# A decode step over a cached window, bound by its loads: sums of half heads, one bank for value products, constants from GpSimd

## The chip, the cores and the metric

The kernel runs on one core of one Trainium2 chip. The metric is device time in microseconds (us) per execution, the median of three runs; a separate execution is profiled. TensorE (PE) multiplies matrices into PSUM, a memory of eight banks with 512 fp32 words per partition each; VectorE (DVE), ScalarE (ACT) and GpSimd (POOL) work elementwise; SyncE (SP) issues nearly all DMAs, in its program's order. Engines wait for each other through semaphores (`wait_ge`).

## What is computed

For a batch of B = 4, one new token each, D = 640, 32 heads of Dh = 192, and the last W = 2048 of 8192 cached positions:

```python
xn  = layernorm(x)
q   = (xn @ wq) per head
k, v = k_cache[:, :, -W:, :], v_cache[:, :, -W:, :]
o   = softmax(q k^T * Dh**-0.5) v          # per batch row and head
out = x + o @ wo + (silu(xn @ w1) * (xn @ w3)) @ w2
```

All inputs are bf16. K and V of the window are 3.1 MB per head each, some 200 MB in all; each element of them is used once.

## The kernel before

**Layout.** The 128 partitions hold 32 groups of positions for each of the 4 batch rows; a head's K tile is 128 x 64 positions x 192. There are two K buffers `kt`, two V buffers `vt`, one buffer `prs` for products of K and q with two halves, and eight PSUM banks: `ps` 0 and 1, `o_ps` 0 and 1, `mt`, `tb`, `po`, `acc`.

**Start.** SP loads W_q (into the V buffers and `prs`), w1, w3, w2, K0 and K1 without waiting (L172 to L179). GpSimd makes two identity matrices (L207 to L213). VectorE makes the constants `one`, `tot_w`, `sel_w`, `mask` (L226 to L243), then the layernorm; through the helper `dv` each of its operations waits for the one before. PE projects q for all heads into six banks, VectorE and ScalarE copy it to `qbc` (L257 to L263, L345 to L348); then come the gated MLP's products, with the gate in `tb` (L405 to L420).

**One head h.** VectorE multiplies K with q in two halves (`mult`, L274), 128 x 6144 each. Per quarter of a head PE adds up the 192 products in six matmuls of 512 columns with the identity (`adder`, L422), which leaves 16 positions x 32 partial sums in one bank, and VectorE sums the 32 (`reduce_quarter`, L280). Then follow for the softmax: the maximum per partition (`chain_lmax`, L285), a transpose on PE (`tr`, L434), the maximum per batch row (`chain_gmax`, L289), its negative on ScalarE (L353), a matmul that spreads it over the partitions (`bc`, L438), its copy and the exponential with row sums on ScalarE (L355, L357), the weights times a batch mask (`chain_z`, L294), a matmul that sums the row sums (`tot`, L443), and 32 matmuls with V (`pv`, L447). ScalarE copies the value product out (L360); `osum` (L458) collects it into `po`, two heads together, and VectorE scales it by the reciprocal (`norm_rec` and `norm_og`, L299 and L302), for every second head. `proj` (L464) multiplies by W_o into `acc`.

**Order.** Every engine's order is written out by hand. On VectorE, per head h (L310 to L325): `mult(h,0)`, the last two quarters of head h-1, `lmax(h-1)`, `mult(h,1)`, `gmax(h-1)`, the first two quarters of head h, for odd heads the reciprocal and the scaling of an earlier pair, `z(h-1)`. On PE, per head (L489 to L498): `adder(0)`, `tr(h-1)`, `osum(h-2)`, `adder(1)`, `bc(h-1)`, `adder(2)`, `tot(h-1)`, `pv(h-1)`, `adder(3)`. The first and third `adder` wait for a reduce that follows the product on VectorE (`s_pr`). The heads at both ends are written out (L470 to L483 and L501 to L543).

**Loads.** SP alternates K(h+2) and V(h+1) (L181 to L183). K(h+2) waits until both products of head h are made (`s_m`, L159), V(h+1) until the value product of head h-1 is made (`s_pv`, L165). The last ones are K30, K31, V29, V30, V31 in two parts (L190 to L194), and behind them the last rows of W_o, into the first K buffer, in four pieces, the last of them 160 KB (L195 to L200).

Of the kernel before, what the change touches and what calls it, by code (L numbers as in the profile page):

```python
# [16 lines left out]
def kernel(  # L17
# [95 lines left out]
    ps = [psum(f"ps{i}", [P, QC], FP32) for i in range(2)]  # L113
    o_ps = [psum(f"o_ps{i}", [P, QC], FP32) for i in range(2)]
    mt = psum("mt", [P, QC], FP32)
    tb = psum("tb", [P, QC], FP32)
# [3 lines left out]
    def sem(name):  # L120
# [4 lines left out]
     s_gp, s_dv, s_ac, s_pp, s_m, s_ps, s_red, s_tr, s_gmax, s_bc, s_negm, s_exp, s_pv, s_sum, s_rec, s_og, s_oT,  # L125
     s_tot, s_acc) = [sem(n) for n in (
        "s_x", "s_wq0", "s_wq1", "s_wq2", "s_w1", "s_w3", "s_w2", "s_k0", "s_k1", "s_v31", "s_wom", "s_wo5",
        "s_wo6", "s_wo7a", "s_wo7b", "s_gp", "s_dv", "s_ac", "s_pp", "s_m", "s_ps", "s_red", "s_tr", "s_gmax", "s_bc",
# [28 lines left out]
    def load_k(h):  # L157
        if h >= 2:
            sp.wait_ge(s_m, 2 * (h - 2) + 2)  # L159
        sp.dma_start(out=flat(kt[h % 2]), in_=k_win[:, h].rearrange("b (p j) d -> p b (j d)", p=PB)).then_inc(s_k[h % 2], 16)  # L160
# [34 lines left out]
    sp.wait_ge(s_m, 2 * (H - 2) + 2)  # L195
# [18 lines left out]


# [3 lines left out]
    def dv(fn, *a, **k):  # L219
        if n_dv[0]:  # L220
            ve.wait_ge(s_dv, n_dv[0])
        fn(*a, **k).then_inc(s_dv, 1)  # L222
        n_dv[0] += 1
        return n_dv[0]

    dv(ve.memset, one[:], 1.0)  # L226
    dv(ve.memset, tot_w[:], 0.0)
    dv(ve.memset, sel_w[:], 0.0)
    dv(ve.memset, acc[:, 0:N0], 0.0)
# [3 lines left out]
    dv(ve.tensor_reduce, out=rows[:], in_=idf[:].rearrange("q (c k) -> q k c", k=CT)[:, 0:2 * B, :], axis=AX.X, op=ALU.add)  # L233
    PQ = CT // B

    def quads(t, par):
        return t.rearrange("p (s q r) b -> p s q r b", s=2, q=2)[:, :, par]

    for par in range(2):
        dv(ve.tensor_copy, out=quads(tot_w[:, par], par), in_=mask_f[:].unsqueeze(1).unsqueeze(1).to_broadcast([P, 2, PQ, B]))  # L240
        for k in range(2):
            dv(ve.tensor_copy, out=quads(sel_w[:, par, k], par),
               in_=rows[:, k * B:(k + 1) * B].unsqueeze(1).unsqueeze(1).to_broadcast([P, 2, PQ, B]))  # L243
    ve.wait_ge(s_x, 16)
    dv(ve.tensor_copy, out=xf, in_=x_sb[:])
# [4 lines left out]
    n_vpe = dv(ve.tensor_scalar, out=vpe[:], in0=ssq[:], scalar1=1.0 / D, scalar2=EPS, op0=ALU.mult, op1=ALU.add)  # L250
    ve.wait_ge(s_ac, 2)
    dv(ve.reciprocal, out=rstd[:], in_=std[:])
    n_xn = dv(ve.tensor_scalar_mul, out=xn[:], in0=xc, scalar1=rstd[:, 0:1])
    xnT_ps = tb[:, 0:KC * B // 2].bitcast(BF16).rearrange("p (k b) -> p k b", b=B)
    ve.wait_ge(s_pp, 1)
    n_xnT = dv(ve.tensor_copy, out=xnT[:], in_=xnT_ps.unsqueeze(2).to_broadcast([P, KC, PB, B]))
    q_banks = [ps[0], ps[1], o_ps[0], o_ps[1], mt, tb]  # L257
    n_qd = []
    for c0 in (0, 6):
        for i in (1, 3, 5):  # L260
            ve.wait_ge(s_pp, 1 + c0 + i + 1)
            n = dv(ve.tensor_copy, out=qbc[:, (c0 + i) * QC:(c0 + i + 1) * QC], in_=q_banks[i][:])
        n_qd.append(n)  # L263
    ve.wait_ge(s_ac, 2 + 6)
    for i in range(2):
        dv(ve.memset, o_ps[i][:, 0:2 * Dh], 0.0)
# [3 lines left out]
       in1=sT[:].rearrange("p (r c) -> p r c", c=FC), op=ALU.mult)  # L270
    n_hT = dv(ve.transpose, out=flat(hT), in_=flat(hb))

    def mult(h, a):
        if a == 0:  # L274
# [3 lines left out]
                         op=ALU.mult).then_inc(s_m, 1)  # L278

    def reduce_quarter(h, g):  # L280
        ve.wait_ge(s_ps, GQ * h + g + 1)
        ve.tensor_reduce(out=sc[h % 3][:, g * JQ:(g + 1) * JQ], in_=ps[g % 2][:].rearrange("p (j d) -> p j d", d=DD),  # L282
                         axis=AX.X, op=ALU.add).then_inc(s_red if g % 2 else s_pr, 1)
# [15 lines left out]
    def norm_rec(i):  # L299
        ve.reciprocal(out=rt[:], in_=tb[:, 0:1]).then_inc(s_rec, 1)  # L300

    def norm_og(i):  # L302
        sl = slice(i % 2 * 2 * CT, (i % 2 + 1) * 2 * CT)
        ve.wait_ge(s_rec, i + 1)
# [5 lines left out]
    for h in range(H):  # L310
        mult(h, 0)
        if h:
            reduce_quarter(h - 1, 2)
            reduce_quarter(h - 1, 3)
# [4 lines left out]
        reduce_quarter(h, 0)  # L319
        reduce_quarter(h, 1)  # L320
        if h % 2 and h > 1:
            norm_rec(h // 2 - 1)
            norm_og(h // 2 - 1)
        if h:
            chain_z(h - 1)  # L325
    reduce_quarter(H - 1, 2)
    reduce_quarter(H - 1, 3)
# [4 lines left out]
    norm_rec(NP - 1)  # L332
    ve.wait_ge(s_sum, H)
# [11 lines left out]
    for c0 in (0, 6):  # L345
        for i in (0, 2, 4):
            ae.wait_ge(s_pp, 1 + c0 + i + 1)
            ae.copy(out=qbc[:, (c0 + i) * QC:(c0 + i + 1) * QC], in_=q_banks[i][:]).then_inc(s_ac, 1)  # L348
    ae.wait_ge(s_pp, 14)
    ae.activation(out=sT[:], in_=tb[:, 0:FW], func=ACTF.Silu).then_inc(s_ac, 1)  # L350
    for h in range(H):
# [8 lines left out]
        ae.copy(out=o_sb[h % 2][:], in_=o_ps[h % 2][:, 0:2 * Dh]).then_inc(s_osb, 1)  # L360
# [28 lines left out]
    acc_add(idb[0:B, 0:B], x_sb[:], start=True)  # L389
    pe.wait_ge(s_dv, n_xnT)  # L390
    for c0 in (0, 6):
# [3 lines left out]
        for kc in range(KC):  # L395
# [4 lines left out]
            for i, qp in enumerate(q_banks):  # L400
                m = held(qp[:], w, wq_rows[kc][:, (c0 + i) * QC:(c0 + i + 1) * QC], kc == 0, kc == KC - 1)
# [3 lines left out]
    for t, bank, s in ((wts[0], tb, s_w1), (wts[1], mt, s_w3)):  # L405
        if bank is tb:
            pe.wait_ge(s_dv, n_qd[1])
        else:
            pe.wait_ge(s_ac, 2 + 6)
# [12 lines left out]
    def adder(g):  # L422
        if g % 2 == 0:
            take(pe, s_pr)
        add_up(g)

    def add_up(g):
        pe.ldweights(idb[:])  # L428
        pr = prs[:, g // 2, g % 2]
        for kk in range(NK):  # L430
            m = held(ps[g % 2][:].rearrange("p (j d) -> p j d", d=DD), idb[:], pr[:, :, kk * DD:(kk + 1) * DD], kk == 0, kk == NK - 1)
# [142 lines left out]
```

## Time and profile before

| what | before |
|---|---|
| median of 3 runs | 528.28 us (528.25 to 528.38) |
| the profiled execution | 528.51 us |
| its span | 525.7 us |
| DMA | 223.08 MB, mean 424 GB/s |
| PE busy | 358.6 us (68%), 2307 matmuls |
| VectorE busy | 342.0 us (65%), 360 instructions |
| ScalarE busy | 54.2 us (10%) |
| GpSimd busy | 1.1 us, 8 instructions |
| products of K and q (L276) | 64 x 3353 ns |
| sums of a quarter on VectorE (L282) | 128 x 681 ns |
| granted TensorE clock, mean | 0.86 |

The span is cut into 40 equal slices in the page; each digit of a strip is a busy share in tenths. A group's line gives the source line, engine, operation, the tiles it writes and reads, how often, the busy time, and the time that its engine sat idle ahead of it with what ended the idleness. A line of the timeline begins with start and duration in us. Where PE is busy at a low granted clock, the same matmuls take longer, so its busy time is no measure of its work.

### The profile page before, as it was taken

How to read it: one execution, taken by the hardware profiler on the slowest of the kernel's cores; microseconds unless marked ns; L12 is line 12 of the kernel's file. 1: busy time of each engine (PE TensorE's matmuls, PEld its weight loads, DVE VectorE, ACT ScalarE, POOL GpSimd, SP SyncE). 2: the span in 40 equal slices, each digit the busy share in tenths (PEclk: the TensorE clock that was granted, in tenths of full speed). 3: DMA queues.
4: the chain of work that ended last, by engine and by line, in shares of the span. 5: the costliest groups of instructions: out<-in, count | busy, mean ns of one | idle time of the engine just before them, and what ended most of it. 6: DMA issues, size and time to landing. Idle time of an engine off the chain costs nothing. (4 is left out here: it accounts for less than half of the span.)

```text
span 525.7 us, 4915 instructions
## 1 busy us (share of the span) xinstructions
PE 358.6 (68%) x2307; PEld 98.3 (19%) x1617; DVE 342.0 (65%) x360; ACT 54.2 (10%) x174; POOL 1.1 (0%) x8
## 2 busy tenths in 40 slices
PE   2664786667587267866767666877676667678697
PEld 0010121112121012211112111222121112222133
DVE  4135777777367574668767676667776766667961
ACT  2120110000111011110100111111010101111010
POOL 0000000000000000000000000000000000000000
PEclk9997888878869688797878888788797888887999
DMA  8999999999999999999999999999999999999995
GB/s 358 422 440 423 438 428 434 434 426 426 439 438 428 434 422 442 428 439 425 439 425 439 428 438 428 434 432 430 438 426 441 426 435 430 438 428 434 432 419 211
DMA packets 11521, 223.08 MB, mean 424 GB/s; under 512 B 1260, under 2 KB 1400, under 8 KB 2424
## 3 DMA queue, kind: packets, MB, share of 16 engines
q1 hardware_dynamic: 11496, 222.96, 98.8%
q8 instruction: 4, 0.07, 0.0%
q14 instruction: 5, 0.04, 0.0%
q10 hardware_dynamic: 16, 0.01, 0.0%
HBM read 222.96 MB, written 0.01 MB: 424 GB/s over the span
## 5 line engine op out<-in xcount | busy, mean ns | idle before, releaser
L374 PE MATMUL ps<-prs,idb 128*128 128x512 bf16 x768 | 225.8, 439 | 136.7 <-PEq L137 129.8
L276 DVE TENSOR_TENSOR prs<-kt,qbc 128x6144 bf16<-128x6144 bf16 x64 | 214.5, 3353 | 110.4 <-DMA kt<-in_A_k_cache_dram 110.4
L282 DVE TENSOR_REDUCE sc<-ps 128x16 f32<-128x512 f32 x128 | 84.2, 681 | 28.1 <-PE ps L374 27.9
L428 PEld LDWEIGHTS <-idb 128*128 128x128 bf16 x128 | 13.4, 105 | 195.2 <-issue 184.2
L460 PE MATMUL po<-o_sb,sel_w 128*128 128x192 f32 x128 | 49.4, 520 | 0.7 <-PEq L137 0.7
L452 PE MATMUL o_ps<-vt,z 128*8 128x384 bf16 x1024 | 47.2, 326 | 1.6 <-PEq L137 1.6
L353 ACT ACTIVATE gneg<-gmax 1x128 f32<-1x128 f32 x32 | 9.8, 308 | 303.5 <-DVE gmax L291 303.5
L460 PEld LDWEIGHTS po<-o_sb,sel_w 128*128 128x128 f32 x128 | 32.9, 284 | 12.6 <-issue 8.3
L452 PEld LDWEIGHTS o_ps<-vt,z 128*8 128x8 bf16 x1024 | 22.0, 86 | 16.0 <-issue 3.2
L360 ACT COPY o_sb<-o_ps 128x384 f32<-128x384 f32 x32 | 15.3, 479 | 89.2 <-PE o_ps L452 89.2
L440 PEld LDWEIGHTS mt<-one,gneg 1*128 1x128 f32 x64 | 9.4, 182 | 63.2 <-issue 63.2
L296 DVE TENSOR_TENSOR z<-ex,mask_b 128x256 bf16<-128x256 bf16 x32 | 13.1, 411 | 7.6 <-ACT ex L357 7.6
L445 PEld LDWEIGHTS tb<-rsum,tot_w 128*128 128x128 f32 x64 | 9.5, 188 | 44.3 <-issue 44.3
L445 PE MATMUL tb<-rsum,tot_w 128*128 128x1 f32 x64 | 11.3, 246 | 4.2 <-PEq L137 4.1
L436 PEld LDWEIGHTS mt<-idf,lmax 128*1 128x1 f32 x32 | 3.7, 116 | 51.5 <-issue 51.5
L440 PE MATMUL mt<-one,gneg 1*128 1x1 f32 x64 | 11.9, 253 | 1.8 <-PEq L137 1.7
L222 DVE CAST qbc<-ps 128x512 bf16<-128x512 f32 x2 | 1.4, 692 | 17.3 <-PE ps L374 17.3
L436 PE MATMUL mt<-idf,lmax 128*1 128x128 f32 x32 | 12.5, 389 | 0.0
L357 ACT ACTIVATE ex<-sc,negm 128x64 bf16<-128x64 f32 x32 | 11.1, 348 | 1.0
L291 DVE TENSOR_REDUCE gmax<-mt 1x4 f32<-1x128 f32 x32 | 8.7, 272 | 1.5 <-PE mt L436 1.5
L355 ACT COPY negm<-mt 128x1 f32<-128x1 f32 x32 | 5.1, 159 | 44.1 <-PE mt L440 44.1
L305 DVE TENSOR_SCALAR og<-po,rt 64x192 bf16<-64x192 f32 x16 | 6.7, 416 | 4.0 <-PE po L460 3.5
(69 smaller groups left out, 86.4 us busy)
## 6 DMA issues: line engine op xcount, KB each, us to landing
kt<-in_A_k_cache_dram SPq DMA_DIRECT2D x32, 3072.0 KB, 21.0
vt<-in_A_v_cache_dram SPq DMA_DIRECT2D x31, 3072.0 KB, 23.4
vt<-in_A_wq_dram SPq DMA_DIRECT2D x2, 3072.0 KB, 13.4
wt<-in_B_w_dram SPq DMA_DIRECT2D x3, 1920.0 KB, 28.0
wt<-in_A_wo_dram SPq DMA_DIRECT2D x2, 1920.0 KB, 29.7
vt<-in_A_v_cache_dram SPq DMA_DIRECT2D x2, 1536.0 KB, 10.8
kt<-in_A_wo_dram SPq DMA_DIRECT2D x2, 960.0 KB, 14.7
prs<-in_A_wq_dram SPq DMA_DIRECT2D x1, 1536.0 KB, 20.0
```

What stands on the lines that cost most here:

```text
L276: ve.tensor_tensor(out=prs[:, a].rearrange("p q j d -> p (q j) d"), in0=kt[h % 2][:, 2 * a * JQ:2 * (a + 1) * JQ, :], in1=qbc[:, h * Dh:(h ...
L282: ve.tensor_reduce(out=sc[h % 3][:, g * JQ:(g + 1) * JQ], in_=ps[g % 2][:].rearrange("p (j d) -> p j d", d=DD), axis=AX.X, op=ALU.add).the ...
L296: ve.tensor_tensor(out=z[h % 2][:], in0=ex[h % 2][:].unsqueeze(2).to_broadcast([P, NJ, B]), in1=mask_b[:].unsqueeze(1).to_broadcast([P, NJ ...
L357: ae.activation(out=ex[h % 2][:], in_=sc[h % 3][:], func=ACTF.Exp, bias=negm[h % 2][:, 0:1], scale=SCALE, accum_out=rsum[h % 2][:]).then_i ...
L360: ae.copy(out=o_sb[h % 2][:], in_=o_ps[h % 2][:, 0:2 * Dh]).then_inc(s_osb, 1)
L374: return pe.add_instruction(mybir.InstMatmult(name=nc.get_next_instruction_name(), engine=pe.engine, ins=[pe.lower_ap(rhs), pe.lower_ap(lh ...
L428: pe.ldweights(idb[:])
L436: pe.transpose(out=mt[0:1, 0:P], in_=lmax[par][:], identity=idf[:]).then_inc(s_tr, 1)
L440: pe.matmul(mt[:, P:P + 1], lhsT=flat(gneg[par]), rhs=one[:], start=True, stop=True).then_inc(s_bc, 1)
L445: return pe.matmul(tb[:, 0:1], lhsT=flat(tot_w[:, par]), rhs=rsum[par][:], start=(par == 0), stop=(par == 1))
L452: m = pe.matmul(o_ps[par][c * CT:c * CT + 2 * B, 0:2 * Dh].rearrange("p (a d) -> p a d", a=2), lhsT=z[par][:, 2 * jj:2 * jj + 2, :], rhs=v ...
L460: m = pe.matmul(po[:, 0:Dh], lhsT=flat(sel_w[:, par, k]), rhs=o_sb[par][:, k * Dh:(k + 1) * Dh].rearrange("p (r i) -> p i r", i=RPP), star ...
```

## The change

1. `ps` becomes one tensor of four banks, two for each half of a head. PE sums a half head (12 matmuls, two banks) behind one wait, and VectorE sums it in one instruction of 128 x 1024 (`reduce_half`).
2. PE waits for the product itself (`s_pr` is now raised by `mult`; `s_m` is gone). K's reload waits for the reduce of the first half (`s_red`), which VectorE does behind `mult(h,1)` and `gmax(h-1)`.
3. The order on PE becomes `adder(0)`, `tr`, `osum`, `bc`, `adder(1)`, `tot` (for two heads at once, at every second head), `pv`.
4. `o_ps` is one bank instead of two; `tb` is gone: `tot` goes into a column of `mt`, the gate and the transposed input into `po`.
5. The reciprocal stands ahead of `lmax` and waits for `s_pv`; the scaling waits for `s_sum`.
6. GpSimd clears and fills `tot_w` and `sel_w`; PE waits for that before the projection of q. Many of VectorE's waits for its own previous operation are dropped (`own=False`).

```diff
-    ps = [psum(f"ps{i}", [P, QC], FP32) for i in range(2)]
-    o_ps = [psum(f"o_ps{i}", [P, QC], FP32) for i in range(2)]
+    ps = psum("ps", [P, 2, 2, QC], FP32)
+    o_ps = psum("o_ps", [P, QC], FP32)
     mt = psum("mt", [P, QC], FP32)
-    tb = psum("tb", [P, QC], FP32)
...
     def load_k(h):
         if h >= 2:
-            sp.wait_ge(s_m, 2 * (h - 2) + 2)
+            sp.wait_ge(s_red, 2 * (h - 2) + 1)
...
-    sp.wait_ge(s_m, 2 * (H - 2) + 2)
+    sp.wait_ge(s_red, 2 * (H - 2) + 1)
...
+    gp.memset(tot_w[:], 0.0).then_inc(s_gp, 1)
+    gp.memset(sel_w[:], 0.0).then_inc(s_gp, 1)
...
+    gp.wait_ge(s_dv, 3)
+    for par in range(2):
+        for t, src in ((tot_w[:, par], mask_f[:]), (sel_w[:, par, 0], rows[:, 0:B]), (sel_w[:, par, 1], rows[:, B:2 * B])):
+            gp.wait_ge(s_gp, 6)
+            gp.tensor_copy(out=quads(t, par), in_=src.unsqueeze(1).unsqueeze(1).to_broadcast([P, 2, PQ, B])).then_inc(s_gp, 1)
...
-    def reduce_quarter(h, g):
-        ve.wait_ge(s_ps, GQ * h + g + 1)
-        ve.tensor_reduce(out=sc[h % 3][:, g * JQ:(g + 1) * JQ], in_=ps[g % 2][:].rearrange("p (j d) -> p j d", d=DD),
-                         axis=AX.X, op=ALU.add).then_inc(s_red if g % 2 else s_pr, 1)
+                         op=ALU.mult).then_inc(s_pr, 1)
+
+    def reduce_half(h, a):
+        ve.wait_ge(s_ps, 2 * h + a + 1)
+        ve.tensor_reduce(out=sc[h % 3][:, 2 * a * JQ:2 * (a + 1) * JQ], in_=ps[:, a].rearrange("p q (j d) -> p (q j) d", d=DD),
+                         axis=AX.X, op=ALU.add).then_inc(s_red, 1)
...
     for h in range(H):
+        odd = h % 2 and h > 1
         mult(h, 0)
         if h:
-            reduce_quarter(h - 1, 2)
-            reduce_quarter(h - 1, 3)
+            reduce_half(h - 1, 1)
+            if odd:
+                ve.wait_ge(s_pv, h - 1)
+                norm_rec()
             chain_lmax(h - 1)
         mult(h, 1)
         if h:
             chain_gmax(h - 1)
-        reduce_quarter(h, 0)
-        reduce_quarter(h, 1)
-        if h % 2 and h > 1:
-            norm_rec(h // 2 - 1)
+        reduce_half(h, 0)
+        if odd:
             norm_og(h // 2 - 1)
...
+    pe.wait_ge(s_gp, 12)
     pe.wait_ge(s_dv, n_xnT)
...
-    def adder(g):
-        if g % 2 == 0:
-            take(pe, s_pr)
-        add_up(g)
...
+    def adder(a):
+        take(pe, s_pr)
         pe.ldweights(idb[:])
-        pr = prs[:, g // 2, g % 2]
-        for kk in range(NK):
-            m = held(ps[g % 2][:].rearrange("p (j d) -> p j d", d=DD), idb[:], pr[:, :, kk * DD:(kk + 1) * DD], kk == 0, kk == NK - 1)
+        for q in range(2):
+            for kk in range(NK):
+                m = held(ps[:, a, q].rearrange("p (j d) -> p j d", d=DD), idb[:], prs[:, a, q, :, kk * DD:(kk + 1) * DD],
+                         kk == 0, kk == NK - 1)
         m.then_inc(s_ps, 1)
...
     with pe.While(lambda: pe.snap(cnt) < NP - 1):
         for par in range(2):
             adder(0)
             tr(1 - par)
             osum(par)
+            bc(1 - par)
             adder(1)
-            bc(1 - par)
-            adder(2)
-            tot(1 - par)
+            take(pe, s_z)
+            if par == 0:
+                tot()
             pv(1 - par)
-            adder(3)
```

The written-out heads at both ends are changed in the same way; in the last pair `tot` of both heads stands ahead of `pv(1, 0, NJ // 2)`.

## Prediction

> **What bounds the kernel now.** I read the page's DMA strips first, then SP's own waits, then the end in order of time.
>
> ```profile
> DMA  8999999999999999999999999999999999999995
> q1 hardware_dynamic: 11496, 222.96, 98.8%
> ```
>
> The DMA strip has no thin slice between the first and the last: the one queue that carries the caches keeps the 16 engines busy 98.8% of the span. Over 62 to 512 us the table by stretches gives 432 GB/s. So 223 MB set the time, and an edit counts only if it starves this queue or lies behind its end. The views of waits (SP's own, then all; total us, times, longest) say whether it is near starving, and the view of the K tile how long a load takes from issue to landing:
>
> ```profile
> SPq L160 <- DVE prs L276: 289.5, 30, 18.7
> SPq L168 <- PE o_ps L452: 144.6, 29, 15.7
> DMA to landing us min/median/max: 13.7/21.0/46.5
> DVE prs L276 <- DMA kt<-in_A_k_cache_dram: 110.4, 30, 8.9
> ```
>
> SP waits for a free buffer before nearly every load, but one K load (3.146 MB) takes only 3.146/0.432 = 7.3 us on the engines. Landing 21.0 us after its issue means 13.7 us of earlier transfers were queued; the tightest one, K31, still had 13.7 - 7.3 = 6.4 us ahead of it. VectorE sits idle 110.4/30 = 3.7 us a head until K lands. All three engines have slack in the middle; the time beyond DMA is at the end. The timelines of PE and VectorE there:
>
> ```profile
> 499.98 1.47 PE L452 MATMUL o_ps<-vt,z 128*8 128x384 bf16 x32 [1.57 <-PEq L137]
> 501.38 1.47 PE L374 MATMUL ps<-prs,idb 128*128 128x512 bf16 x6
> 502.69 0.27 PE L436 MATMUL mt<-idf,lmax 128*1 128x128 f32 x1
> 502.80 1.52 PE L460 MATMUL po<-o_sb,sel_w 128*128 128x192 f32 x4
> 504.14 1.48 PE L374 MATMUL ps<-prs,idb 128*128 128x512 bf16 x6
> 505.55 0.38 PE L440 MATMUL mt<-one,gneg 1*128 1x1 f32 x2
> 505.86 1.47 PE L374 MATMUL ps<-prs,idb 128*128 128x512 bf16 x6
> 507.34 0.35 PE L445 MATMUL tb<-rsum,tot_w 128*128 128x1 f32 x2
> 507.56 1.46 PE L374 MATMUL ps<-prs,idb 128*128 128x512 bf16 x6
> 508.94 1.47 PE L452 MATMUL o_ps<-vt,z 128*8 128x384 bf16 x32
> ...
> 515.83 0.38 PE L445 MATMUL tb<-rsum,tot_w 128*128 128x1 f32 x2
> ...
> 519.80 2.61 PE L386 MATMUL acc<-kt,oT 128*4 128x320 bf16 x36
> ```
> ```profile
> 498.87 1.28 DVE L282 TENSOR_REDUCE sc<-ps 128x16 f32<-128x512 f32 x2
> 500.18 0.22 DVE L287 TENSOR_REDUCE lmax<-sc 128x1 f32<-128x64 f32 x1
> 500.32 3.35 DVE L276 TENSOR_TENSOR prs<-kt,qbc 128x6144 bf16<-128x6144 bf16 x1
> 503.58 0.27 DVE L291 TENSOR_REDUCE gmax<-mt 1x4 f32<-1x128 f32 x1
> ```
>
> PE starts the value product of head 29 at 499.98, when V29 lands, and from there works without a gap (only 0.68 us, the copy of the last value product, stays empty) to 522.4. The last transfer (wo7b) is issued at 504.96 and lands 16.4 us later, at 521.4. PE thus ends 1.0 us behind DMA: **PE's work after V29 sets the end**, and DMA is a floor some 0.8 us below it (two matmuls follow that landing).
>
> **The change, part by part.** The profiled execution took 528.51 us: a span of 525.7 and 2.8 around it. The median of the runs is 528.28, 0.23 lower; sums are made on the profile and then lowered by that.
>
> 1. *One sum per half head.* Two reduces of 512 take 1.28 us together (0.69 alone). From gmax (128 elements, 0.272) and the mean of the page's reduce (512, 0.681) an element costs 1.065 ns, so 1024 cost 0.681 + 0.545 = 1.23. No row has a reduce over two banks: from below 1.07 (1024 elements, no fixed part), from above 2 x 0.69 = 1.38; I take 1.23, the slope. 64 x 0.05 = 3 us less of VectorE, hidden by the 3.7 us it waits for K per head: 0. If K ceased to be late, that would be the gain.
>
> 2. *Earlier start of the sums on PE.* The adder waits for the product alone and no longer for a reduce behind it: at 474.90 PE started 0.75 us after the product's end (470.80 + 3.36). Now it starts at once, but the transpose stands behind 12 matmuls and bc ahead of the second half. In the middle this moves the value product of a head from 14.4 us (485.2 - 470.8) to some 15 us behind K's landing; V loads wait for that with V's predecessors still queued. 0.
>
> 3. *K's reload waits for the reduce of the first half, not the second product.* Behind the product (ends 8.1 us after K's landing, 475.53 + 3.35 - 470.80) now come gmax, 0.27, and a reduce, 1.23; where PE is slow (six sums in 2.5 us, 474.90 to 477.41), 12 take 5.1 and gmax waits about 1 us more. So each K load is issued 1.4 to 2.5 us later, and V's behind it in SP's order at most as much. K31's 6.4 us of queue shrink to 3.9; from issue to first bytes took 1.1 us at the start (issued 0.96, flowing in the row of 2 to 3 us). No gap: 0. Head 0: the first reduce ends at about 53.1 (PE had two quarters summed at 51.9) instead of K2's issue at 50.87, and V0 occupies DMA until K2's landing less one transfer, 65.82 - 7.3 = 58.5. 0. The final wo loads wait for the same counter, reached near 495; they are issued behind V31 at 502.7 anyway. 0.
>
> 4. *One bank for value products.* pv(h) must follow the copy of pv(h-1); osum, ahead of it on PE, waits for that copy already. 0.
>
> 5. *Constants on GpSimd, VectorE's own waits dropped.* GpSimd gets two memsets and six copies behind its last row (ends 2.06). Memsets of 128 columns take 0.43 start to start: 256 and 512 columns cost from 0.4 to 2.6; six copies of 64 columns from 0.6 (0.1 each, its smallest row) to 1.8 (0.3 each, its select). Done at 3.1 to 6.5; I take 6. PE asks at 11.2 or, with VectorE freed of 1.5 us, at 9.7, and anyway idles for W_q (1.80 us before 18.30). Even a lateness past that would only eat VectorE's 6.83 us of idle before K0 lands at 44.2. 0, and the 1.5 us earlier norm and the 1.5 us earlier gate matmul are worth 0 for the same reason.
>  The Trainium skill (GPSIMD Engine Reference, § 2.1 Instruction dispatch) speaks against this part: a first call to a freshly loaded library kernel pays about 6 us that no row shows. No row here shows such a pause; by that rule the constants would be ready near 12 us, an estimate from that page, and the sum would still be 0 by the waits for W_q and K0.
>
> 6. *The end.* Here the order counts. Head 31 is odd, so VectorE now takes the reciprocal between the reduce of head 30 and its lmax, behind a new wait for pv(29), which ends at 501.4 because V29 landed at 499.9. Queued behind this wait: lmax(30), the product (31,1), gmax(30); PE's tr and bc wait for those. VectorE would be there at 498.87 + 1.23 = 500.1, so it stands 1.3 us; reciprocal 0.16, lmax; product from 501.8 to 505.15 (was 500.32 to 503.67), gmax at 505.06 (0.09 before, as in the rows), gneg 0.31 later, bc 0.42 after that (493.75 to 494.17 at head 29): **505.79**. PE meanwhile: 12 sums from 501.38 at 1.31 per six (to 502.69) = 504.00, tr 0.11, osum 1.34: free at **505.45**. So 1.48 us of delay shrink to 0.34 us of idle PE. Then bc 0.31, 12 sums 2.62 to 2.86 (the rows' six take 1.31 to 1.48): 508.72 to 508.96, against 508.94 before. The tot of head 30 (507.34 to 507.56, 0.22) is gone from this place and stands doubled at 515.83, 0.31 more. Result: -0.22 to +0.02, plus 0.31: **+0.1 to +0.3 us**, middle 0.2. What follows (pv(31), copy, osum, 36 projections) is the same.
>  The row before that: head 30's sums start behind an idle of about 3.4 us (2.95 before, and the six then took 1.46; after 4.20 idle they took 2.72). Slow sums there push z(29) by at most 0.7 us and the product (31,0) with it, to 500.8 with its reduce, still ahead of pv(29)'s end: 0. The Trainium skill (TensorE: Matmul & The Clock Gate, § Part 1: The HAM clock gate) says that an idle window of about 3.4 us halves the clock; 2.95 and 4.20 agree with it, and by it these sums would be slow, which the last sentence prices at 0.
>
> Sum: 528.51 + 0.2 = 528.7 on the profile's scale, **528.5 us** on that of the runs.
>
> **Rivals.**
> - *Slower: the reciprocal's wait is not absorbed at the end.* For it: it puts the product (31,1) behind V29's landing, and nothing after it is idle. Against it: 4.07 us of PE's own work lie between. With no absorption, +1.48 + 0.31 - 0.22 = +1.6: 529.9. It decides past the 0.2% (1.06 us, about what a measurement here can tell from no change), from an idle of about 1.1 us before bc(30) instead of 0.34, say if the release of the wait and the chain behind it take 0.8 us longer than the rows.
> - *Slower: DMA starves because K is asked for later.* It needs a delay over 6.4 - 1.1 = 5.3 us at K31, or 6.5 at K2; I find 2.5. One such gap of 2 us, less the 0.8 of floor: +1.2 to +2, 529.5 to 530.3.
> - *Faster.* If PE's end shortened, the floor gives at most -0.8: 527.5, still within 0.2%. More needs faster DMA: 2 to 22 us moved 415 GB/s where 432 follow, 20 x (1 - 415/432) = 0.8 us. If VectorE's or GpSimd's early work caused that and it went, with the floor reached: 526.7. Nothing in the profile ties the two.
> - *The change doesn't shorten the sum* (1.38 for two banks): VectorE 6 us more, hidden by K: the forecast's time.
>
> **How the numbers follow.** Forecast, with the floor and the useless sum: 0.80. Reciprocal not absorbed: 0.10. Starved DMA: 0.04. Faster DMA: 0.06. So faster 0.06, same 0.80, slower 0.14. The range takes the forecast's bounds from the floor's 527.4 and reaches into the first rival, to 529.6.
>
> **What would show it.** Right: the DMA strip as flat as before; reduces of 128x1024 near 1.23 us; K loads issued about 1.5 to 2.5 us later after landing; a wait of about 1.3 us before the last but one reciprocal; PE idle 0.2 to 0.5 us before bc(30); two tots in a row near 516; PE's end near 522.6. Wrong: a slice of the DMA strip under 9 in the middle, V31 issued after 502, a half-speed PE behind 500, or a last landing well ahead of 521.

## The result, and the profile after

| | before | after |
|---|---|---|
| median | 528.15 us (528.01 to 528.46, 10 runs) | 526.83 us (526.71 to 527.79, 10 runs) |
| profiled execution | 528.51 us | 526.78 us |
| its span | 525.66 us | 524.93 us |
| time around the span | 2.85 us | 1.85 us |
| sums on VectorE | 128 x 681 ns | 64 x 1211 ns |
| VectorE instructions in the program (in the trace) | 387 (383) | 302 (298) |

The ratio is 0.9975, with an interval of 0.9967 to 0.9983: faster by a quarter of a per cent. The forecast was 528.5, and the time lies below its range. Of the 1.73 us between the two profiled executions 0.73 lie in the span and 1.00 around it, that is in the time of an execution ahead of its first instruction and behind its last. The medians are 1.32 us apart.

The strip and the queues of the page after (queue, kind: packets, MB, share of 16 engines):

```profile
DMA  8999999999999999999999999999999999999995
q1 hardware_dynamic: 11496, 222.96, 98.9%
q8 instruction: 4, 0.07, 0.0%
q14 instruction: 4, 0.03, 0.0%
```

and the same two queues in the page before:

```profile
q8 instruction: 4, 0.07, 0.0%
q14 instruction: 5, 0.04, 0.0%
```

The strip is as flat as it was, and the caches move at the same rate. The line that differs is the last: the engines' programs come through the same DMA engines, and there is one packet less. The prediction made nothing of that line, which stands there with 0.0%.

SP's own waits after:

```profile
SPq L159 <- DVE sc L281: 310.3, 30, 19.9
SPq L167 <- PE o_ps L448: 123.0, 29, 16.5
```

K's reload now waits for the reduce, 310.3 us where the product cost 289.5, and V's wait shrinks by about as much: the landings below show that no load is late for it. The end on PE and on VectorE, after:

```profile
498.26 0.98 PE L385 MATMUL acc<-wt,oT 128*4 128x320 bf16 x12
499.29 1.47 PE L448 MATMUL o_ps<-vt,z 128*8 128x384 bf16 x32
500.69 2.76 PE L373 MATMUL ps<-prs,idb 128*128 128x512 bf16 x12
503.30 0.27 PE L431 MATMUL mt<-idf,lmax 128*1 128x128 f32 x1
503.40 1.52 PE L456 MATMUL po<-o_sb,sel_w 128*128 128x192 f32 x4
505.04 0.35 PE L435 MATMUL mt<-one,gneg 1*128 1x1 f32 x2
505.32 2.76 PE L373 MATMUL ps<-prs,idb 128*128 128x512 bf16 x12
...
514.90 0.61 PE L440 MATMUL mt<-rsum,tot_w 128*128 128x1 f32 x4
...
519.10 2.61 PE L385 MATMUL acc<-kt,oT 128*4 128x320 bf16 x36
```
```profile
499.60 1.22 DVE L281 TENSOR_REDUCE sc<-ps 128x32 f32<-128x1024 f32 x1
500.81 0.17 DVE L299 RECIPROCAL rt<-mt 128x1 f32<-128x1 f32 x1
500.90 0.20 DVE L286 TENSOR_REDUCE lmax<-sc 128x1 f32<-128x64 f32 x1
501.01 3.35 DVE L275 TENSOR_TENSOR prs<-kt,qbc 128x6144 bf16<-128x6144 bf16 x1
504.28 0.27 DVE L290 TENSOR_REDUCE gmax<-mt 1x4 f32<-1x128 f32 x1
```

From the value product of head 29 to PE's end it takes 521.71 - 499.29 = 22.42 us; before it took 522.41 - 499.98, the same to 0.01. So the tail costs what it cost, and the whole gain in the span is that this tail starts 0.69 us earlier: **V29 lands earlier**, at 499.15 instead of 499.84 us. PE has only just come free then (its projection ends at 499.24), so with a still earlier V29 PE itself would be the limit there. The same shows 29 us before the end, where VectorE waits for K29 and starts its product the moment it lands. Before, and then after:

```profile
470.80 3.36 DVE L276 TENSOR_TENSOR prs<-kt,qbc 128x6144 bf16<-128x6144 bf16 x1 [3.40 <-DMA kt<-in_A_k_cache_dram]
```
```profile
470.08 3.36 DVE L275 TENSOR_TENSOR prs<-kt,qbc 128x6144 bf16<-128x6144 bf16 x1 [3.43 <-DMA kt<-in_A_k_cache_dram]
```

For each load the trace records 16 increments of its semaphore, at 16 times; I read each as the landing of the share that one of the 16 DMA engines moves. For K29 the ninth of the sixteen comes at 468.42 us before and at 468.43 after. The last comes at 470.77 before and at 470.06 after. So DMA as a whole is no faster. **One engine of the sixteen is less far behind**: its lag behind the ninth, followed from load to load before, goes from 1.46 to 2.45 us near 425 us, while the last but one stays at 1.4 to 1.5, and is still 2.33 at V29; after it is 1.62 there. In that stretch the queues of before are (425 is inside it):

```profile
q1 hardware_dynamic: 67, 1.25, 98.3%
q14 instruction: 1, 0.01, 0.6%
```

A packet of 8 KB of VectorE's program arrives there, and the full engine that carries it does not get the time back. VectorE's packets come at 42, 246 and 425 us before, when it has executed about 47, 178 and 306 instructions, so one for each 128; after, at 89 and 324 us (50 and 175 instructions), and the third would be due at about 303, behind the 298 that it executes. (The queue's two other packets, near 138 and 507 us, are there in both and come at the same points of ScalarE's program.)

### The profile page after: what moved, and what is told of

Read it like the earlier page. It is cut to its first block, busy times and chain, and to the rows that moved or that the text cites. A ratio compares the mean times of both kernels' runs of the same rounds, so it can differ in the third digit from the quotient of the medians.

```text
span 524.9 us, 4774 instructions
## 1 busy us (share of the span) xinstructions
PE 366.4 (70%) x2306; PEld 83.7 (16%) x1553; DVE 334.6 (64%) x287; ACT 54.1 (10%) x174; POOL 3.4 (1%) x16
## 5 line engine op out<-in xcount | busy, mean ns | idle before, releaser
L373 PE MATMUL ps<-prs,idb 128*128 128x512 bf16 x768 | 229.0, 461 | 134.1 <-PEq L136 134.1
L281 DVE TENSOR_REDUCE sc<-ps 128x32 f32<-128x1024 f32 x64 | 77.5, 1211 | 3.3 <-PE ps L373 3.1
L422 PEld LDWEIGHTS <-idb 128*128 128x128 bf16 x64 | 6.3, 98 | 153.1 <-issue 152.6
L456 PEld LDWEIGHTS po<-o_sb,sel_w 128*128 128x128 f32 x128 | 25.3, 221 | 14.7 <-issue 5.2
L440 PEld LDWEIGHTS mt<-rsum,tot_w 128*128 128x128 f32 x64 | 9.6, 191 | 35.1 <-issue 34.7
L234 DVE CAST qbc<-ps 128x512 bf16<-128x512 f32 x4 | 2.6, 686 | 19.7 <-PE ps L373 19.7
L373 PE MATMUL ps<-vt,xnT 128*128 128x512 bf16 x31 | 10.6, 477 | 5.0 <-DMA vt<-in_A_wq_dram 3.9
L435 PEld LDWEIGHTS mt<-one,gneg 1*128 1x128 f32 x64 | 9.4, 182 | 22.4 <-issue 22.4
L431 PE MATMUL mt<-idf,lmax 128*1 128x128 f32 x32 | 10.5, 328 | 0.0
L440 PE MATMUL mt<-rsum,tot_w 128*128 128x1 f32 x64 | 8.1, 231 | 0.0
```

The source lines that it names most:

```text
L281: ve.tensor_reduce(out=sc[h % 3][:, 2 * a * JQ:2 * (a + 1) * JQ], in_=ps[:, a].rearrange("p q (j d) -> p (q j) d", d=DD), axis=AX.X, op=AL ...
L373: return pe.add_instruction(mybir.InstMatmult(name=nc.get_next_instruction_name(), engine=pe.engine, ins=[pe.lower_ap(rhs), pe.lower_ap(lh ...
L431: pe.transpose(out=mt[0:1, 0:P], in_=lmax[par][:], identity=idf[:]).then_inc(s_tr, 1)
L435: pe.matmul(mt[:, P:P + 1], lhsT=flat(gneg[par]), rhs=one[:], start=True, stop=True).then_inc(s_bc, 1)
L440: m = pe.matmul(mt[:, P + 1:P + 2], lhsT=flat(tot_w[:, par]), rhs=rsum[par][:], start=(par == 0), stop=(par == 1))
L456: m = pe.matmul(po[:, 0:Dh], lhsT=flat(sel_w[:, par, k]), rhs=o_sb[par][:, k * Dh:(k + 1) * Dh].rearrange("p (r i) -> p i r", i=RPP), star ...
```

## The experiments

The first question was whether the gain comes from the code's packets or from the work that the change removes. All ratios are to the kernel before on the same chip, with 95% intervals. A range of spans is over all executions of a run; landings are those of its profiled execution.

**The kernel before, unchanged**, as a measure of what a difference is worth.

> The kernel before, unchanged, to have its span and its time in several executions and not in one. Theory A (code fetches: the packets that load the engines' instructions share the 16 full DMA engines, and a block fetched behind the end lies outside the span): time 528.2, span 525.4 to 525.8, so 2.4 to 2.8 outside the span in most executions, with code packets near 42 us and near 527. Theory B (the gain comes from the work itself: earlier start, less VectorE work, other order of loads): the part outside the span is chance and scatters between 1.9 and 2.8, as little as in the changed kernel.

528.69 us, ratio 1.0002 (0.9993 to 1.0011). Spans 525.7 to 526.3, K29 at 470.87. In 9 of its 11 executions over 2.1 us lie around the span.

**The changed kernel with 12 weight loads on PE**, which brings PE's program back to its length before.

> The changed kernel with 12 more weight loads of the identity on PE, in its idle time before K0 lands, so that PE's program is as long as before (1083 instructions instead of 1071). They do no work that anything waits for. Theory A: span as in the changed kernel, 524.9 to 525.2, but PE's last code block is fetched again behind the end: 0.6 to 0.9 more outside the span, time 527.5 to 527.8. Theory B: 526.8, nothing outside the span changes.

```diff
+    for _ in range(12):
+        pe.ldweights(idb[:])
     adder(0)
     adder(1)
```

526.92 us, ratio 0.9969 (0.9957 to 0.9981); 1.79 to 1.87 around the span in each execution. The length of PE's program explains nothing.

**The changed kernel with 85 one-element memsets on VectorE**, which brings its program back to 387 instructions at almost no work.

> The changed kernel with 85 memsets of one element on VectorE (25 before K0 lands, 2 per head up to head 29), so that VectorE's program is as long as before (387 instructions instead of 302), all in time in which it waits for K. Theory A: a third code packet for VectorE in the middle of the run; it delays one DMA engine by 0.3 to 1.0, and the span grows by 0.3 to 0.8 if this is one of the slowest, 0 if it is not: 526.8 to 527.6, the gain in the span partly gone; outside the span 1.9 as in the changed kernel. Theory B: 526.8, since all sums, orders and constants are those of the changed kernel.

```diff
+    idle = sb("idle", [1, 512], BF16)
...
+    def pad(n):
+        for _ in range(n):
+            ve.memset(idle[:, n_idle[0]:n_idle[0] + 1], 0.0)
+            n_idle[0] += 1
...
+    pad(25)
...
+        pad(2 if h < H - 2 else 0)
```

528.53 us, ratio 0.9997 (0.9988 to 1.0006): the gain is gone. VectorE's packets come at 42, 236 and 416 us, at 53, 178 and 303 instructions, K29 lands at 471.10 and V29 at 500.17. The ninth engine has K29 at 468.68 us, 0.25 later than in the changed kernel; the rest of the delay is the last engine's lag. That is the code theory's case; but the span, 526.0 to 527.0, exceeds before's, and around the span there are mostly 1.8 us, not before's 2.5 and more, so the equality in the sum is partly chance. PE ends 1.88 us later than in the changed kernel, and V29 accounts for 1.02 of it; the rest comes behind V31, whose first half is late, and PE waits 0.70 us for the last rows of W_o.

**The kernel before with 12 instructions less on PE** (a quarter of the gated MLP's last product is left out).

> The kernel before without the last three of twelve column groups of the product with w2 (6 of 24 matmuls with their weight loads, in PE's idle time before K0; a quarter of the gated MLP is left out of the output), so that PE's program is as short as in the changed kernel (1071). Theory A: span 525.4 to 525.8 as before, outside it 1.9 instead of 2.8: 527.3 to 527.7. Theory B: 528.2, since nothing on the path changes.

```diff
-    for c in range(FC):
+    for c in range(FC - 3):
         m = acc_add(hT[:, c, 0:B], wts[2][:, c * D:(c + 1) * D])
```

528.80 us, ratio 1.0001 (0.9992 to 1.001), span and surroundings as before. PE's program is out from this side too.

**The changed kernel with V29 asked for ahead of K31.** The tail hangs on V29, so why not load it sooner?

> The changed kernel, with V29 asked for ahead of K31 instead of behind it. If the end is set by PE's work after V29's landing (22.42 us of it in both traces), V29 lands 7 us earlier and PE's end moves forward until the next thing is late: the last transfer lands at about 520.7 in the changed kernel's trace, and two matmuls and the output follow. Expected then: span 524.1 to 524.5, time 526.0 to 526.4 with 1.85 us around the span, a ratio to the kernel before of 0.995 to 0.996. If instead the end is set by DMA's slowest engine all along, nothing moves: 526.8. If K31, now 7 us later, takes V29's place (its product is 8 us of VectorE ahead of the last value products), the time grows to 528 or more.

```diff
-        if h < H - 4:
+        if h < H - 3:
             load_v(h + 1)
...
-    load_v(H - 3)
     load_v(H - 2)
```

531.36 us, ratio 1.0051 (1.0038 to 1.0065), the case named last in the expectation. PE:

```profile
498.98 1.54 PE L447 MATMUL o_ps<-vt,z 128*8 128x384 bf16 x28
502.68 4.32 PE L372 MATMUL ps<-prs,idb 128*128 128x512 bf16 x12 [2.15 <-PEq L136]
```

K31 takes V29's place at 499.15, its first product starts at 499.18 and PE idles 2.15 us for it, then sums slowly. The view of waits of the kernel before names one load as the one that ends the idleness; it doesn't say how soon the next one binds.

**The kernel before with part 5 alone** (constants on GpSimd, fewer waits on VectorE).

> The kernel before with part 5 of the prediction alone: TensorE's constants made by GpSimd, VectorE's own waits dropped. VectorE's program is 19 instructions shorter than before's, GpSimd's 9 longer. Code theory: VectorE still executes past its third packet's place (at about 306 instructions), only some 20 instructions, 2 heads, later: the packet comes at about 455 us instead of 425, and the span keeps before's 525.7 to 526.3; with the packet at 42 us gone K0 may land earlier, which buys nothing. Work theory (the gain lies in the constants): span 524.9. Around the span: if what GpSimd has to run decides it, 1.85 in every execution, so 527.6 to 528.0 in all, ratio 0.9985; if not, 2.8 in most of them and 528.6.

528.41 us, ratio 1.0 (0.9991 to 1.0009). The third packet comes at 451 instead of 425 us, K29 lands at 470.96: part 5 alone buys nothing, as forecast, in the span or around it (over 2.1 us in 8 of 11 executions).

**The kernel before with nine memsets on GpSimd.**

> The kernel before plus nine one-element memsets on GpSimd, as many instructions as part 5 adds there (31 becomes 40); nothing else moves. If the length of GpSimd's program decides the time around the span, that is 1.85 us in every execution and no code packets come behind the span's end: 527.6 to 528.1, ratio 0.9985. If the constants themselves, the missing semaphore or VectorE's program do, it stays at 2.5 to 3.4 in most executions, with a 16 KB and an 8 KB packet 1.8 us behind the end: 528.6. The span stays at 525.7 to 526.4 by either theory.

```diff
...
+    for i in range(9):
+        gp.memset(idle[:, i:i + 1], 0.0)
```

528.55 us, ratio 1.0004 (0.9995 to 1.0013); over 2.1 us around the span in all 11. GpSimd's length is not what decides that.

**The changed kernel without part 5.** The constants are back on VectorE with all its waits, as in the code before; 322 VectorE instructions.

> The changed kernel without part 5: VectorE makes the constants and keeps its own waits, as in the kernel before. VectorE's program is 20 instructions longer than the changed kernel's, 65 shorter than before's; GpSimd's is before's. Code theory: the third VectorE packet's place, about 306 instructions, is reached only at the last head if at all, too late to delay V29: span 524.9 to 525.2. If part 5 made the span shorter, 525.7. Around the span: 2.8 in most executions if GpSimd's program decides that (527.8 in all, ratio 0.998), 1.85 if the halved sums, the missing semaphore or the shared bank do (526.9, ratio 0.9965).

526.83 us, ratio 0.9972 (0.996 to 0.9984), the time of the changed kernel; median span 525.0, though the profiled one, 525.6, exceeds the expectation. VectorE's packets come at 47 and 289 us and not a third one before K29, which lands at 470.19, nor before V29, at 499.27. Part 5 is worth nothing in this direction either.

**The changed kernel with part 1 undone alone**: the same waits and orders, but two instructions per half.

> The changed kernel with part 1 undone alone: each half is summed by two instructions of 512 again, after the same one wait and with the same releases. VectorE executes 362 instructions instead of 298 and spends about 3 us more. Code theory: the third code packet comes at about instruction 306, near 430 to 455 us, the lag at V29 goes from 1.5 to 2.4 us, and the span is 525.7 to 526.5, like the 85 memsets. If the third packet isn't what counts: 524.9 to 525.2, since 3 us of VectorE are hidden by its idle time before K. Around the span 1.85 as in the changed kernel, so 527.6 to 528.4 or 526.8 in all.

```diff
-        ve.tensor_reduce(out=sc[h % 3][:, 2 * a * JQ:2 * (a + 1) * JQ], in_=ps[:, a].rearrange("p q (j d) -> p (q j) d", d=DD),
-                         axis=AX.X, op=ALU.add).then_inc(s_red, 1)
+        for q in range(2):
+            g = 2 * a + q
+            n = ve.tensor_reduce(out=sc[h % 3][:, g * JQ:(g + 1) * JQ], in_=ps[:, a, q].rearrange("p (j d) -> p j d", d=DD),
+                                 axis=AX.X, op=ALU.add)
+        n.then_inc(s_red, 1)
```

528.49 us, ratio 0.9998 (0.999 to 1.0007); median span 526.6. The third packet is at 452 us, and K29:

```profile
471.02 3.36 DVE L275 TENSOR_TENSOR prs<-kt,qbc 128x6144 bf16<-128x6144 bf16 x1 [4.00 <-DMA kt<-in_A_k_cache_dram]
```

The idle time ahead of it, 4.00 us, says that VectorE was early, not late: the 3 us of extra sums are not what delays the load. The span is longer than the code theory's 525.7 to 526.5 in half of the executions, and the trace shows a second cause. K31's issue and PE's last rows:

```profile
481.54 0.54 SPq L159 DMA_DIRECT2D kt<-in_A_k_cache_dram  x1
```
```profile
522.30 0.98 PE L388 MATMUL acc<-kt,oT 128*4 128x320 bf16 x12 [0.57 <-DMA kt<-in_A_wo_dram]
```

K31 is asked for at 481.54, 2.1 us later than in the changed kernel, and the ninth engine has it at 491.38 instead of 490.26: here DMA starved for 1.1 us. (V29 lands at 500.00 for that reason: its last share is only 1.36 us behind its ninth. The packet's part is seen at K29.) What follows arrives later by that and by another 0.8 us at the first half of V31, and PE waits for the last rows of W_o.

**The changed kernel with 400 memsets on VectorE**: a dose.

> The changed kernel with 400 one-element memsets on VectorE, 40 in the prelude and 12 in each head up to the 29th: some 698 instructions, so five code packets ahead of V29 instead of two, and some 25 us of VectorE more, under 1 us a head beside 4 us of idle time before K. Code theory: what a packet costs depends on whether it falls to the engine that is already last. If all fall to one, the lag at V29 grows by 0.3 to 1.0 us each, to 2.5 to 4.5 us, and the span to 526 to 528; if they rotate, the lag stays at that of three packets, 2.5, and the span at 525.7 to 526.8. Rival: a third packet is a step and not a cost each, 525.7 to 526.3; or packets don't count, 524.9.

530.22 us, ratio 1.003 (1.0018 to 1.0042); spans 528.1 to 528.4. K29:

```profile
472.90 3.36 DVE L284 TENSOR_TENSOR prs<-kt,qbc 128x6144 bf16<-128x6144 bf16 x1 [3.86 <-DMA kt<-in_A_k_cache_dram]
```

Between 110 and 420 us this program fetches five packets on that queue, one of them ScalarE's:

```profile
q1 hardware_dynamic: 6596, 134.02, 100.5%
q14 instruction: 5, 0.04, 0.0%
```

The last engine's lag is 1.49 us ahead of VectorE's packet at 118 us, and 2.09, 2.91, 3.75 and 4.58 us behind those at 118, 224, 312 and 404 us, while the ninth engine has K29 at 468.41, as in the kernel before. From the load ahead of a packet to the load behind it three of the four add 0.98 to 0.99 us each, of which 0.1 to 0.2 is lost again until the next packet, all on the engine that is last already. It is a cost per packet, not a step. (K31 is issued at 482.43 and DMA starves as in the run before. That too follows from the packets: the issue comes 9.55 us behind K29's landing, where it comes 9.38 behind it in the changed kernel, and K29 lands 2.8 us later.)

**The changed kernel with the end delayed.**

> The changed kernel with three sums of 512 on VectorE (results unused) between the last projection and the copy of the result: the end comes 1.6 to 2.2 us later, everything before it is unchanged, so the span is 526.5 to 527.2. The question is the time around the span. If only the moment of the end decides whether it is 1.85 or 2.5 to 3.4, as V29 ahead of K31 made it appear (2.4 to 3.0 in three of five, with the changed kernel's programs on all engines but SP's order), some of these executions show 2.5 or more; if not, all show 1.85.

```diff
...
     ve.wait_ge(s_acc, 1)
+    for i in range(3):
+        ve.tensor_reduce(out=late[:, i:i + 1], in_=qbc[:, i * QC:(i + 1) * QC], axis=AX.X, op=ALU.add)
     ve.tensor_copy(out=res[:], in_=acc[0:CT + B, 0:N0]).then_inc(s_fin, 3)
```

528.77 us, ratio 1.0005 (0.9996 to 1.0013), spans 526.6 to 527.6, 1.80 to 1.88 around the span in all 11 executions. A later end by itself does not lengthen what lies around it.

**The kernel before with a shorter VectorE program**: the reverse test, first try.

> The kernel before with part 5 and without the normalisation (reciprocal, scaling, transpose) of heads 0 to 27, whose rows of the projection are zeros here. VectorE executes about 329 instructions instead of 383, sums in quarters as before and on two banks as before: nothing of the halved sums is in it. Code theory: the place of VectorE's third code packet (instruction 306) is reached only behind 500 us, at the time V29 lands or later, so the slowest DMA engine lags 1.4 to 1.7 us behind the median at V29 instead of 2.4, V29 lands at about 499.3 to 499.5 instead of 499.98 and the span is 524.9 to 525.2. If the halved sums themselves made the gain in the span, it stays at 525.7 to 526.3. Around the span: 2.5 to 3.4 in most executions if it goes with the order of the end (which is before's), 1.85 if it goes with VectorE's packets.

```diff
...
-        if h % 2 and h > 1:
+        if h % 2 and h // 2 > SKIP:
             norm_rec(h // 2 - 1)
             norm_og(h // 2 - 1)
...
```

528.80 us, ratio 0.9997 (0.9987 to 1.0008): its forecast of V29 missed. Up to 492 us it went as the code theory says: two packets, K29 at 470.33, K31 at 492.15 (492.57 before). But the third packet came at 498.19, not behind 500, the lag went to 2.8 us, and V29, in flight just then, landed at 500.40, later than in the kernel before. The cost was moved to the one load that can't bear it. The value product behind V29 then ran slow (2.66 us instead of 1.47), and the tail took 24.07 us. Half of the executions have spans of 525.5 to 526.3 us and half 527.5 to 527.9; the profile is one of the latter.

**The same with four instructions less**, so that the packet falls behind V29.

> The kernel before, sums in quarters, with the normalisation of heads 0 to 27 left out as in the run before it with a shorter VectorE program, and four instructions of VectorE's prelude moved or dropped (one and mask_b made by GpSimd, x read without a copy, the epsilon added by ScalarE), so that VectorE's third code packet comes behind the product (31,0) and the sums of head 30, near 503 us instead of 498. Code theory: nothing hits the queue between 300 and 500 us, so K31 lands near 492.1, V29 near 499.3 to 499.4 (499.84 to 500.0 in the kernel before, 500.40 with the packet at 498), PE's end comes 22.4 us later and the span is 524.9 to 525.4, with quarter sums and nothing of the halved ones. If the halved sums are needed for the gain: V29 near 499.9, span 525.7 or more. Around the span 1.85 or 2.8; no theory stands behind either.

```diff
-    dv(ve.tensor_copy, out=mask_b[:], in_=mask_f[:])
+    gp.tensor_copy(out=mask_b[:], in_=mask_f[:]).then_inc(s_gp, 1)
...
-    dv(ve.memset, one[:], 1.0, own=False)
+    gp.memset(one[:], 1.0).then_inc(s_gp, 1)
...
-    dv(ve.tensor_copy, out=xf, in_=x_sb[:], own=False)
...
-    n_vpe = dv(ve.tensor_scalar, out=vpe[:], in0=ssq[:], scalar1=1.0 / D, scalar2=EPS, op0=ALU.mult, op1=ALU.add, own=False)
...
```

527.58 us, ratio 0.9986 (0.9977 to 0.9995): faster than before, with sums in quarters. No packet moves on the code queue of VectorE and ScalarE between 300 and 506 us. K29 lands at 470.10, K31 at 491.94, V29 at 499.19: the landings of the changed kernel, as expected, so the halved sums are not needed for them. But PE's end, 522.17, came 22.84 us behind the start of its value product instead of 22.4, and the median span was 525.7, not 524.9 to 525.4 (the kernel before has 525.9 on the same chip, so most of this run's gain lies around the span):

```profile
488.80 2.72 PE L378 MATMUL ps<-prs,idb 128*128 128x512 bf16 x6 [4.33 <-PEq L137]
...
505.39 0.35 PE L445 MATMUL mt<-one,gneg 1*128 1x1 f32 x2 [0.43 <-PEq L137]
```

Head 30's sums stand behind an idle of 4.33 us, run slowly (2.72 us for six instead of 1.47), push the weights of head 29 and with them both products of head 31, and PE then waits 0.43 us for `gneg`. Another 0.35 us went between PE's end and the copy of the result (0.46 instead of 0.11); no run explains it.

**The changed kernel with K31 in two halves, V29 between them.**

> The changed kernel with K31 loaded in two halves and V29 between them: first half of K31, V29, second half of K31, V30. V29 then lands half a K load (3.6 us) earlier, at about 495.5, the second half of K31 at 499.2, before the place at which VectorE can take up the product (31,1) today (501.0). V29 whole ahead of K31 cost 4.5 us, because the product (31,0) then waited for 499.2; here only the second product needs that landing. Expected: PE's end moves forward until DMA's last landing (520.7) is the limit, 521.0 to 521.3 instead of 521.7, so a span of 524.2 to 524.6 and a time of 526.0 to 526.4, ratio 0.9955. If the half loads move slower than whole ones, or the second product is late all the same: 526.8 or more.

```diff
...
+    sp.wait_ge(s_red, 2 * (H - 3) + 1)
+    half_k(H - 1, 0, NJ // 2, s_k[1])
     load_v(H - 3)
+    half_k(H - 1, NJ // 2, NJ, s_k31)
     load_v(H - 2)
...
```

527.17 us, ratio 0.9979 (0.9968 to 0.9989); spans 524.6 to 525.3, their median 524.9 where the changed kernel has 525.0: short of the expected gain. V29 landed at 495.62 as planned, and then the end was DMA's:

```profile
518.08 1.80 PE L397 MATMUL acc<-kt,oT 128*4 128x320 bf16 x24
520.47 0.98 PE L397 MATMUL acc<-kt,oT 128*4 128x320 bf16 x12 [0.60 <-DMA kt<-in_A_wo_dram]
```

PE waits 0.60 us for the last rows but one piece and ends at 521.45 instead of 521.71. With the last landing at 520.7 there is only a quarter of a microsecond left to win behind V29, and the surroundings of the span took more than that back (over 2.1 us in 4 of 8). No version tried beats the changed kernel.

**Around the span.** This part of the gain, 1.00 of the 1.73 us, stays open. What the runs show:

| kernel | executions with over 2.1 us around the span | code packets behind the span's end in the profile |
|---|---|---|
| before, unchanged, on four chips | 78 of 98 | two, at +1.8 and +2.1 us |
| before, PE less 12 / constants / GpSimd 9 | 9 of 11 / 8 of 11 / 11 of 11 | two / one at +2.1 / two |
| after | 0 of 10 | none |
| after, PE 12 / no constants / late end | 0 of 6 / 0 of 6 / 0 of 11 | none / one at +1.1 / none |
| after, 85 memsets / quarters / 400 memsets | 3 of 11 / 2 of 11 / 2 of 6 | none |
| after, V29 first / K31 halves | 3 of 5 / 4 of 8 | two, at +1.8 to +2.3, in each |
| before, shorter VectorE, first try / second | 1 of 12 / 1 of 11 | none / one at +1.8 |

In each of the seven profiles without such a packet 1.82 to 1.89 us lie around the span, in each with one at about 1.8 us or later 2.04 to 3.3. The profile before, the stretch from 526 to 530 us, where nothing but two packets moves:

```profile
q8 instruction: 1, 0.02, 2.0%
q14 instruction: 1, 0.01, 0.8%
```

Whether these packets make the execution longer or are only caught by a longer one, the runs don't tell. The lengths of the programs don't decide it by themselves: V29 ahead of K31 and K31 in halves leave VectorE's and PE's instruction counts as they are after, and bring the packets back. The Trainium skill (Runtime: NRT & Kernel Launch, § Instruction fetch mechanics) says that a branch to code outside the fetched window forces a fetch; that would suit packets behind a program's end, but no run here shows such a branch.

## Why the prediction was wrong

- *What bounds the kernel.* "An edit counts only if it starves this queue or lies behind its end": this is **the step that failed**, and with it the zero that step 1 drew from it. An edit that shortens an engine's program does neither and counts all the same, because a load has landed when the slowest of its 16 shares has, and the program's packets run on the same full engines. From the profile it could have been worked out: VectorE's third packet comes at about its 306th instruction, and the changed program ends ahead of that. What it is worth, 0.7 us, could not have been read from the page's shares, only from the engines' own landings. By itself this would not have taken the time out of the range: 528.51 less the 0.70 us by which PE's end moved, and less the 0.23 us from the profile to the median, is 527.6. What did is the time around the span, below.
- *The chain behind V29* was read rightly: PE's work after V29 set the end in both kernels, 22.42 us.
- *Steps 1 to 4.* The sum takes 1.211 us (1.23 forecast). That and the earlier sums are hidden, as said: undoing part 1 alone leaves 4 us of VectorE's idle time ahead of K29. Its effect came through the number of its instructions, 64 of the 85 that are gone, which the step did not price.
- *Step 3 and the rival of starving DMA* had the right outcome from a wrong margin, and so in part by luck. K31 was asked for 9.38 us after K29's landing instead of 8.13, 1.25 later (1.4 to 2.5 forecast), but the landing itself was 0.7 earlier, so the issue moved by 0.54 only. The point of starving was put at a delay of 5.3 us. By the issues and the ninth engine's landings of K31 in five profiles it is 1.5:

| K31 issued at | 478.9 (before) | 479.44 (after) | 480.68 (no constants) | 481.54 (quarters) | 482.43 (400 memsets) |
|---|---|---|---|---|---|
| ninth engine has it at | 490.25 | 490.26 | 490.66 | 491.38 | 492.11 |

 Past about 480.4 the landing follows the issue at a distance of 9.7 to 10.0 us. The 13.7 us that I subtracted from counted the slowest engine's lag (2.3 us) as queue, and a load's way from issue to first bytes as 1.1 us where 9.8 - 7.3 = 2.5 are left. After, 1.0 us of it was left; with quarters, 2.1 us later, DMA did run dry.
- *Step 5.* The constants were ready by 4.6 us (at most 6 forecast), with copies of 0.2 to 0.75 us; adding or removing this part alone moves nothing (528.41 and 526.83 us). The pause of about 6 us that the Trainium skill (GPSIMD Engine Reference, § 2.1 Instruction dispatch) gives did not show.
- *Step 6.* The reciprocal was to wait 1.3 us. It did not wait at all: head 30's first sums stood behind an idle of 4.43 us (about 3.4 forecast) and ran slow (5.28 us for twelve), so the product came at 496.33 and its reduce ended at 500.81, when the value product had just ended. That was the case priced at 0, and it cost 0: bc at 505.04 stands behind 0.1 us of idle PE (0.34 forecast), and the tail is as long as before (+0.1 to +0.3 forecast).
- *The rivals.* "Faster" had the size, 0.8, but tied it to the rate of DMA at the start; the rate did not change. The sentence that nothing in the profile ties VectorE's work to DMA was wrong: its code does.
- *The scale.* The sum was made on an execution with 2.85 us around its span, taken as given. 1.00 of the 1.73 us between the two profiles went there, and no step had a term for it; why it went stays open.

## What to carry to other kernels

Where DMA is full, count the program's instructions as traffic: each 128 of VectorE's cost here up to 1.0 us of the one engine that carries their packet, and a load waits for that engine. Look at the sixteen landings of a load, not at their mean, and ask where the packet falls: just ahead of the load that the end hangs on it is worst. And before a load is asked for earlier or later, work out the distance from issue to landing with the queue empty; the margin is what lies beyond it.

## What the runs showed of the hardware

- A packet of VectorE's code is 8 KB and comes once for each 128 instructions that it executes, at about 48, 176 and 304 here; it took about 0.3 us, yet the third one before and three with 400 memsets raised the lag of the last engine by 1.0 us each, while others raised it by 0.1 to 0.6 (at 324 us after, at 118 with 400 memsets). The landings suggest why: there the engine that took the packet was not yet the last. After, the last but one share of a load lands 1.04 us behind the ninth ahead of 324 us, and behind it the last two land 1.61 and 1.74 behind the ninth where the last had been at 1.62, so one engine seems to have gone from 1.04 to 1.74. That VectorE's packets always burden the same engine fits this but is not shown; the trace does not name the engine of a packet. The Trainium skill (Runtime: NRT & Kernel Launch, § Instruction fetch mechanics) speaks of refills of 16 KiB and calls the cost of crossing into the next mostly hidden; with these DMA engines full (98.8%) it isn't, and VectorE's packets are half that size.
- The lag outlives its cause while the queue is full: before, it shrank from 2.45 to 2.33 us in the 72 us up to V29, and with 400 memsets by 0.1 to 0.2 in the 80 to 110 us between two packets. It goes when the queue runs dry: with quarters it fell from 2.47 to 1.36 us at the gap ahead of K31, so the starved load's last share came at 492.74, only 0.17 later than in the kernel before, while its ninth came 1.1 later.
- The length of an idle of PE near 3.4 us doesn't tell whether the sums behind it run at full speed. Ahead of the first sums of heads 29 and 30, idles of 3.6 to 4.7 us left them slow in every profile (six took 2.35 to 2.72 us where 1.47 is full speed, twelve 4.10 to 5.28 where it is 2.76). Those of 2.95 to 3.02 (before, and before with part 5 alone) and of 3.43 and 3.47 us (before with PE less 12, the shorter VectorE program's first try) left six at 1.46 to 1.51, and 3.32 (no constants) left twelve at 2.75; but 3.26 (quarters) and 2.94 (late end) gave 4.26 and 4.22 for twelve, and 2.15 with V29 first gave 4.32.
- In three profiles (85 memsets, no constants, quarters) the first half of V31 comes 0.5 to 1.3 us later behind V30 than in the kernel before (by the ninth shares), although it was issued at most 0.4 us later than there; the cause stays open. With 400 memsets and in the shorter VectorE program's first try it comes 0.8 and 1.5 us later too, but there it was issued 1.7 to 2.1 us later.
